# Moving the low-half subtractions of two MLPs from GpSimd to the vector engine, and keeping one step of weight preparation away from the sums

## The chip, the cores and the metric

One core of one Trainium2 chip runs the whole program. Times are device microseconds of an execution; the kernel before took 695.05 us (median of 3 runs, 694.81 to 695.08). Engines are named as the profile names them: PE (matrix products), PEld (its weight loads), DVE (vector engine), ACT (scalar engine), POOL (GpSimd), SP (issues the DMAs).

## The reference, cut to what is computed

```python
q_pool = q.reshape(B, H, S // 2, 2, D).mean(axis=3)            # B 2, H 8, S 1152, D 64
scores = scale * np.matmul(q_pool, k.transpose(0, 1, 3, 2))
attn = softmax(scores)
x = np.matmul(attn, v)  ->  (1152 tokens, 512)
h = x @ w_in            # 512 x 2048, first layer
g = h * np.tanh(log1p(exp(h)))                                 # Mish
x = g @ w_out           # 2048 x 512
h = x @ w_in2           # second layer
g = np.where(h > 0.0, h, np.exp(np.minimum(h, 0.0)) - 1.0)     # ELU
out = g @ w_out2
```

The products of the MLPs are made to nearly full single precision: each operand is cut into a high half in fp32r, which the PE multiplies fast, and a low half, the operand less its high half. Three products (high·high, low·high, high·low) are summed. The weights arrive as 8-byte words and are turned into single precision on the chip.

## The kernel before, in words

Attention runs first, then both MLPs in one loop (`mlps()`). The order on every engine is the order in which the Python code issues instructions; each engine works its own queue in that order and waits at an instruction until its inputs are there.

The MLPs' work is cut into 96 units, 48 for each layer: a unit is one chunk of 128 hidden columns for one block of 384 tokens. The chunks of a layer fall into three groups (6, 5, 5 in the first layer, 5, 5, 6 in the second), and a group is worked for all three token blocks before the next. Pass `u` of the loop issues, in this order:

- `h_mm(u)` (L174): 12 matmuls for the hidden values of unit u, into a bank A of PSUM.
- `out_mm(u-3)` (L570): the matmuls of unit u-3 into the output banks. In the second layer these are 9 matmuls, three into each of 3 banks.
- `finish(u-3)` (L589): only when unit u-3 is the last of its group and block. The **sums**: the output banks are added to `part` in SBUF (L612, on DVE) or copied there (L603 on ACT, L605 on DVE). The banks B, B, B, C, D are given out in turn, so in the second layer the third bank that the next group needs is the first one that these sums set free. "The sums of pass u" are those issued in pass u.
- `split(u-1)` (L564, second layer): ACT copies `g` to its high half `gh` (L567), POOL subtracts to get the low half `gl` (L568).
- `mish(u)` (L537) in the first layer: ACT makes `gh` and `g` (L542, L543), POOL makes `gl` (L544). `elu(u)` (L549) in the second: ACT makes `x`, `e`, `r` (L555 to L557), then DVE `e` (L559) and DVE `g` (L561).
- The steps of weight pieces that have reached their age (`advance`, L638). A piece is half a chunk's weights, 128 x 512. It is read by DMA in pass t; in pass t+2 ACT scales its words (`rebias`, L119) and POOL clamps them (`clamp`, L123); in pass t+3 DVE runs three **words** instructions (L128, L133, L134); in pass t+4 ACT makes the high half `wh` (L144); in pass t+5 POOL makes the low half `wl` (`rest`, L147).
- `between()` (L628): one left-over addition or subtraction of the first layer's result, on POOL.

When pieces are read is settled by a small planner (L520 to L531): every piece has a latest pass, from its chunk's first use, and pieces are read no closer than 1.5 passes apart unless that latest pass forces it. Pieces for the attention part go through the same class `Weights` in another loop (L481 to L495).

Of the kernel before, what the change touches and what calls it, by code (L numbers as in the profile page):

```python
# [16 lines left out]
ALU = mybir.AluOpType  # L17
# [5 lines left out]
def tile_pool_attention_mish_elu_mlp(  # L23
# [14 lines left out]
    nc = tc.nc  # L38
# [44 lines left out]
    class Weights:  # L83
# [59 lines left out]
            self.h, self.l = (t[:, part * DM:(part + 1) * DM] for t in wt[self.layer, self.c])  # L143
            nc.scalar.copy(self.h, self.f)  # L144

        def rest(self):
            nc.gpsimd.tensor_tensor(self.l, self.f, self.h, op=ALU.subtract)  # L147


    ps = ctx.enter_context(tc.tile_pool(name="ps", bufs=1, space=PSUM))  # L150
# [9 lines left out]
    units = []  # L160
# [25 lines left out]
    def attention():  # L186
        with ExitStack() as st:
# [122 lines left out]
            def qk(s, j):  # L310
                n, i = tiles[s]
                KA, KBt = ks[n]
                Q = qs_t[n]
                sc[s, j] = pt = psum("A")
                c = slice(j * KB, (j + 1) * KB)
                if order[i] is None:
                    cols = slice(NQ * P, NQ * P + P)
                    terms = [(Q[0, 0], KA), (Q[0, 1], KA), (Q[1, 0], KBt), (Q[1, 1], KBt)]
                else:
                    h, t = order[i]  # L320
                    cols = slice(t * P, (t + 1) * P)
                    terms = [(Q[h, 0], (KA, KBt)[h]), (Q[h, 1], (KA, KBt)[h])]
                for x, (qq, kk) in enumerate(terms):
                    nc.tensor.matmul(pt[:, :KB], qq[:, cols], kk[:, c], start=(x == 0), stop=(x == len(terms) - 1))  # L324
# [14 lines left out]
            def exp(s):  # L339
                m = stat[s]  # L340
                nc.scalar.activation(sp[s], sp[s], AF.Exp, bias=m[:, 3:4], scale=1.0, accum_out=m[:, 4:5])  # L341
# [95 lines left out]
            while s < len(tiles) or avs or going:  # L437
                o = s - LAG
                new, old = s < len(tiles), 0 <= o < len(tiles)
                mid = 0 <= s - 1 < len(tiles)  # L440
                now = avs.pop(s, [])
                for j in range(3):
                    if new:
                        qk(s, j)
                    if j == 3:
                        for a in now:
                            av(*a)
                    if s in preps and 1 == j:
                        f, n, g = preps.pop(s)
                        f(n, g)  # L450
                    if old:
                        trans(o, j)
                if 3 == 3:
                    for a in now:
                        av(*a)
                more = left["dve"] and not any(w.age == 3 for w in going)
                if mid:
                    exp(s - 1)
                leave("act")
                if old:  # L460
                    for j in range(3):
                        if j != 1 or not more:
                            probs(o, j, nc.scalar.copy)
                if new:
                    scores(s, 0)
                    scores(s, 1)
                if mid:
                    norm(s - 1)
                if new:
                    scores(s, 2)  # L470
                    top(s)
                leave("dve")
                leave("pool", most=2)
                if old and (1 in [j for _, j in tp]):
                    probs(o, 1, nc.vector.tensor_copy)
                for n, g, kt in now:
                    if kt == KT - 1:
                        tokens(n, g)
                if 2 <= s % NI < 2+2 and s // NI + 1 < n_pairs:
                    pool_q(s // NI + 1, nc.gpsimd, (s % NI - 2,))  # L480
                for w in list(going):  # L481
                    w.age += 1
                    if w.age == 2:
                        w.rebias()
                        w.clamp()
                    elif w.age == 3:
                        w.shift()
                    elif w.age == 4:
                        w.words()
                        if w.x >= NW:  # L490
                            going.remove(w)
                    elif w.age == 5:
                        w.high()
                        w.rest()
                        going.remove(w)  # L495
                for f in loads.pop(s, []):
                    f()
                if pieces and s >= 3 and s % 5 == 3:
                    going.append(Weights(*pieces.pop(0)))
                    going[-1].read()  # L500
                s += 1
# [3 lines left out]
    def mlps():  # L505
        with ExitStack() as st:
# [7 lines left out]
            AHEAD = 3  # L514
# [5 lines left out]
            last, t = [], len(units)  # L520
            for x, y in reversed(loads):
                ahead = 8 if x < NW + NF else 7
                t = min(first_use[x] - ahead + AHEAD * y, t - 1)
                last.append(t)
            last.reverse()
            when, t = [], -100.0
            for (x, y), end in zip(loads, last):
                room = last_use[x - RING] + AHEAD - 3 if x >= RING else 0
                t = end if x < NW + NF else min(end, max(t + 1.5, room))
                assert t >= room or x < NW + NF, (x, y)  # L530
                when.append(t)  # L531
            going, later = [], []
# [4 lines left out]
            def mish(u):  # L537

                h = hs.pop(u)[:, :TB]
                g = tmp("g")  # L540
                gh, gl = g_t[u] = halves()
                nc.scalar.activation(gh, h, AF.Mish)  # L542
                nc.scalar.activation(g, h, AF.Mish)  # L543
                nc.gpsimd.tensor_tensor(gl, g, gh, op=ALU.subtract)  # L544

            def halves():
                return tuple(mp.tile([P, TB], F32R, tag=t, name=t, bufs=AHEAD + 1) for t in ("gh", "gl"))
# [1 line left out]
            def elu(u):  # L549


                h = hs.pop(u)[:, :TB]
                x, e, t = tmp("x", 2), tmp("e", 2), tmp("r", 2)
                g = es[u] = tmp("g")
                nc.scalar.activation(x, h, AF.Relu, scale=-1.0)  # L555
                nc.scalar.activation(e, x, AF.Exp, scale=-1.0)
                nc.scalar.activation(t, x, AF.Tanh, scale=-0.5)  # L557
                yield
                nc.vector.scalar_tensor_tensor(e, e, 1.0, t, op0=ALU.add, op1=ALU.mult)  # L559
                yield  # L560
                nc.vector.tensor_tensor(g, e, h, op=ALU.max)  # L561
                yield

            def split(u):  # L564
                g = es.pop(u)
                gh, gl = g_t[u] = halves()
                nc.scalar.copy(gh, g)  # L567
                nc.gpsimd.tensor_tensor(gl, g, gh, op=ALU.subtract)  # L568

            def out_mm(u):  # L570
                layer, gi, blk, c, first, final = units[u]
# [66 lines left out]
            def advance(age, *steps):  # L638

                for g in list(going):  # L640
                    if g.age == age:
                        for f in steps:
                            getattr(g, f)()
                        if "rest" in steps:
                            going.remove(g)

            acts = {}

            def go(u):
                if u in acts:  # L650
                    next(acts[u], None)

            for u in range(min(0, int(when[0]) - 1), len(units) + AHEAD):
                for g in going:
                    g.age += 1
                w = u - AHEAD
                if 0 <= u < len(units):
                    h_mm(u)
                if 0 <= w < len(units):
                    out_mm(w)  # L660
                if 0 <= w < len(units):
                    finish(w)
                if u - 1 in es:
                    split(u - 1)
                if 0 <= u < len(units):
                    if units[u][0] == 0:
                        mish(u)
                    else:
                        acts[u] = elu(u)
                go(u)  # L670
                advance(5, "rest")
                go(u)
                advance(4, "high")
                go(u)
                advance(2, "rebias", "clamp")
                go(u)
                advance(3, "shift", "words")
                between()
                while loads and when[0] <= u:
                    x, y = loads[0]  # L680
                    if x >= RING and last_use[x - RING] + AHEAD > u + 3:
                        break
                    loads.pop(0)
                    when.pop(0)
                    g = Weights(x, y)
                    assert u + (2 if g.ready else 5) <= first_use[x] + AHEAD * y, (x, y, u)
                    going.append(g)
                    if g.ready:
                        g.age = 3
                    else:  # L690
                        g.read()
                    break
            assert not loads and not going and not later

    with tc.manual_schedule():
        attention()
        mlps()
# [29 lines left out]
```

## Time and profile before

| | us |
|---|---|
| runs shown, median (lowest to highest) | 695.05 (694.81 to 695.08) |
| the profiled execution's own time | 695.86 |
| its span, first to last instruction | 694.0 |
| PE busy | 673.9 (97%) |
| DVE busy | 475.9 (69%) |
| ACT busy | 434.0 (63%) |
| POOL busy | 408.5 (59%) |

The share of an engine is over the whole span, and the stages differ: attention takes the first 282 us, the first layer runs from there to about 476 us, the second to the end. The page's chain of waits, followed back from the last instruction, is 73% PE and 18% DVE. To find where PE is held up one reads the busy time by stretch, then PE's instructions in order of time around the one stretch in which its busy time falls short, then the engine named behind the gap.

### The profile page before, as it was taken

Reading aid. Unit: us, or ns where it says so; the run is one execution under the profiler, and the core shown is the slowest. Engines: PE = TensorE matmul, PEld = TensorE weight load, DVE = VectorE, ACT = ScalarE, POOL = GpSimd, SP = SyncE. Lnnn points to the kernel's source line nnn. Section 1 sums busy time; section 2 is a strip of 40 time slices with the busy share of each in tenths; the row PEclk is TensorE's granted clock in tenths of the full one; section 3 lists DMA queues with packets and bytes.
Section 4 is the critical chain, followed back from the end, with each engine's and each line's share of the span. In section 5 each row is a group of like instructions: output and inputs, shape, how many; then the busy total and the mean of one; then the engine's idle time right before and its main releaser. Section 6 shows DMA issues by size and latency. Waiting matters only on the chain.

```text
span 694.0 us, 11253 instructions
## 1 busy us (share of the span) xinstructions
PE 673.9 (97%) x3976; PEld 582.6 (84%) x3976; DVE 475.9 (69%) x1120; ACT 434.0 (63%) x896; POOL 408.5 (59%) x446
## 2 busy tenths in 40 slices
PE   6799999999999999999999999999999999979997
PEld 4677777777777776899999999999989999969996
DVE  5989889898898885001474455765888888895332
ACT  4898988887888787424354554445766666565442
POOL 3666666564646453624576797897775756664221
PEclk9999999999999999999999999999999999989999
DMA  7322232324140200110232222322222223200111
GB/s 200 100 66 69 65 101 65 111 62 128 62 124 9 89 9 1 62 31 32 91 122 92 63 90 91 92 92 61 91 61 92 92 70 102 72 31 1 46 46 45
DMA packets 47400, 50.79 MB, mean 73 GB/s; under 512 B 20336, under 2 KB 38256, under 8 KB 47344
## 3 DMA queue, kind: packets, MB, share of 16 engines
q1 hardware_dynamic: 47344, 50.08, 23.9%
q8 instruction: 31, 0.51, 0.3%
q14 instruction: 25, 0.20, 0.1%
HBM read 47.71 MB, written 2.36 MB: 72 GB/s over the span
## 4 chain that ended last, share of the span: by engine, by line
PE 73%; DVE 18%; issue 4%; ACT 2%; POOL 2%; DMA 0%; DVEq 0%; POOLq 0%
PE A L181 19%; PE A L324 13%; PE B L587 12%; PE C L378 11%; PE B L353 10%; DVE wf L134 4%; DVE e L559 4%; PE D L587 4%; PE C L587 3%; DVE wf L133 3%; DVE wf L128 2%; PE D L254 1%; DVE sp L330 1%; DVE part L612 1%; DVE g L561 1%
## 5 line engine op out<-in xcount | busy, mean ns | idle before, releaser
L347 POOL TENSOR_SCALAR sp<-sp,stat 128x1152 f32<-128x1152 f32 x72 | 89.3, 1240 | 107.1 <-DVE stat L346 67.4
L181 PE MATMUL A<-XH,wh 128*128 128x384 f32 x384 | 129.6, 337 | 0.0
L181 PE MATMUL A<-XH,wl 128*128 128x384 f32 x384 | 129.4, 337 | 0.0
L181 PE MATMUL A<-XL,wh 128*128 128x384 f32 x384 | 129.3, 337 | 0.0
L330 DVE TENSOR_SCALAR_CACHE_REDUCE sp<-A 128x384 f32<-128x384 f32 x216 | 114.3, 549 | 13.6 <-PE A L324 12.4
L353 PE MATMUL B<-ident,sp 128*128 128x128 f32 x648 | 105.7, 273 | 4.4 <-issue 2.2
L341 ACT ACTIVATE sp<-sp,stat 128x1152 f32<-128x1152 f32 x72 | 90.9, 1263 | 23.5 <-DVE stat L337 22.9
L568 POOL TENSOR_TENSOR gl<-g,gh 128x384 fp32r<-128x384 f32 x48 | 55.3, 1152 | 77.4 <-ACT gh L567 77.4
L353 PEld LDWEIGHTS B<-ident,sp 128*128 128x128 f32 x648 | 81.2, 140 | 13.8 <-issue 3.5
L544 POOL TENSOR_TENSOR gl<-g,gh 128x384 fp32r<-128x384 f32 x48 | 55.2, 1153 | 53.7 <-ACT g L543 53.1
L369 ACT COPY pt<-B 128x384 f32<-128x384 f32 x188 | 81.7, 484 | 7.7 <-PE B L353 6.3
L378 PE MATMUL C<-pt,vr 128*64 128x320 f32 (+1 forms) x576 | 85.1, 418 | 0.9 <-DVE XL L394 0.9
L128 DVE TENSOR_SCALAR wf<-wf 128x512 int32<-128x512 int32 x56 | 39.3, 702 | 66.0 <-POOL wf L123 65.8
L147 POOL TENSOR_TENSOR wl<-wf,wh 128x512 fp32r<-128x512 f32 x56 | 83.6, 1493 | 0.4 <-ACT wh L144 0.2
L559 DVE SCALAR_TENSOR_TENSOR e<-e,r 128x384 f32<-128x384 f32 x48 | 44.9, 935 | 48.1 <-ACT r L557 48.0
L181 PEld LDWEIGHTS A<-XH,wh 128*128 128x128 f32 x384 | 72.7, 189 | 2.5 <-issue 0.5
L181 PEld LDWEIGHTS A<-XL,wh 128*128 128x128 f32 x384 | 72.6, 189 | 2.0
L324 PE MATMUL A<-KA,Q 128*128 128x384 f32 x240 | 73.5, 390 | 0.3 <-DVE KA L259 0.2
L181 PEld LDWEIGHTS A<-XH,wl 128*128 128x128 f32 x384 | 72.6, 189 | 0.0
L324 PE MATMUL A<-KB,Q 128*128 128x384 f32 x240 | 71.1, 379 | 1.2 <-DVE sp L330 1.2
L134 DVE SCALAR_TENSOR_TENSOR wf<-raw,wf 128x512 int32<-128x512 int32 x56 | 68.8, 1228 | 1.9
L542 ACT ACTIVATE gh<-A 128x384 fp32r<-128x384 f32 x48 | 23.7, 493 | 69.6 <-PE A L181 69.6
(115 smaller groups left out, 1358.2 us busy)
## 6 DMA issues: line engine op xcount, KB each, us to landing
raw<-in_moe_w_in_dram SPq DMA_DIRECT2D x32, 512.0 KB, 3.8
raw<-in_moe_w_out_dram SPq DMA_DIRECT2D x32, 512.0 KB, 3.3
vr<-in_v_dram SPq DMA_DIRECT2D x8, 576.0 KB, 3.9
kr<-in_k_dram SPq DMA_DIRECT2D x14, 288.0 KB, 4.2
qr<-in_q_dram SPq DMA_DIRECT2D x7, 512.0 KB, 3.9
out_dram<-part SPq DMA_DIRECT2D x8, 256.0 KB, 2.2
kr<-in_k_dram SPq DMA_DIRECT2D x6, 96.0 KB, 3.1
qr<-in_q_dram SPq DMA_DIRECT2D x2, 256.0 KB, 3.3
```

The lines of the kernel that those rows point to most:

```text
L134: nc.vector.scalar_tensor_tensor(f, self.low, 29, f, op0=ALU.logical_shift_right, op1=ALU.bitwise_or)
L147: nc.gpsimd.tensor_tensor(self.l, self.f, self.h, op=ALU.subtract)
L181: nc.tensor.matmul(pt[:, :TB], w[:, kk * P:(kk + 1) * P], x[:, kk, tk], start=(i == 0), stop=(i == len(terms) - 1))
L324: nc.tensor.matmul(pt[:, :KB], qq[:, cols], kk[:, c], start=(x == 0), stop=(x == len(terms) - 1))
L330: nc.vector.tensor_scalar(sp[s][:, j * KB:(j + 1) * KB], sc.pop((s, j))[:, :KB], SCALE, None, op0=ALU.mult, op1=ALU.max, accum_out=stat[s] ...
L341: nc.scalar.activation(sp[s], sp[s], AF.Exp, bias=m[:, 3:4], scale=1.0, accum_out=m[:, 4:5])
L347: nc.gpsimd.tensor_scalar(sp[s], sp[s], m[:, 6:7], 1.0, op0=ALU.mult, op1=ALU.mult)
L353: nc.tensor.transpose(pt[:, x * P:(x + 1) * P], sp[s][:, c:c + P], ident)
L369: copy(dst, src)
L378: nc.tensor.matmul(acc[n, g][h * D:(h + 1) * D, :w], vs[n][:, h, kt, :], pts[n, g][:, kt, h, :], start=(kt == 0), stop=(kt == KT - 1),)
L559: nc.vector.scalar_tensor_tensor(e, e, 1.0, t, op0=ALU.add, op1=ALU.mult)
L587: nc.tensor.matmul(pt, l, r, start=(first and i == 0), stop=(final and i == 2))
```

## The change

POOL's subtractions inside `mlps()` go to DVE: `gl` in `mish` and in `split`, and `wl` in `rest`. In the attention part `rest` stays on POOL. In the first layer `gl` is issued at the end of a pass; in the second, `g` is issued before `rebias`, `clamp` and the words, with nothing between `e` and `g`. The planner gets a set `full` of passes; a piece whose reading pass falls in it, so that its words would be issued in the pass just ahead of the second layer's sums, is read one pass later if its latest pass allows that.

```diff
-        def rest(self):
-            nc.gpsimd.tensor_tensor(self.l, self.f, self.h, op=ALU.subtract)
+        def rest(self, eng=nc.vector):
+            eng.tensor_tensor(self.l, self.f, self.h, op=ALU.subtract)
...
                     elif w.age == 5:
                         w.high()
-                        w.rest()
+                        w.rest(nc.gpsimd)
...
+            full = {u + AHEAD - 4 for u in range(len(units)) if units[u][5] and units[u][0]}
             for (x, y), end in zip(loads, last):
                 room = last_use[x - RING] + AHEAD - 3 if x >= RING else 0
                 t = end if x < NW + NF else min(end, max(t + 1.5, room))
+                if np.ceil(t) in full and t + 1 <= end:
+                    t = np.ceil(t) + 1.0
...
                 nc.scalar.activation(g, h, AF.Mish)
-                nc.gpsimd.tensor_tensor(gl, g, gh, op=ALU.subtract)
+                yield
+                nc.vector.tensor_tensor(gl, g, gh, op=ALU.subtract)
...
                 nc.scalar.copy(gh, g)
-                nc.gpsimd.tensor_tensor(gl, g, gh, op=ALU.subtract)
+                nc.vector.tensor_tensor(gl, g, gh, op=ALU.subtract)
...
                 if 0 <= u < len(units):
-                    if units[u][0] == 0:
-                        mish(u)
-                    else:
-                        acts[u] = elu(u)
+                    acts[u] = (mish, elu)[units[u][0]](u)
                 go(u)
                 advance(5, "rest")
+                advance(4, "high")
+                if 0 <= u < len(units) and units[u][0]:
+                    go(u)
+                    go(u)
+                advance(2, "rebias", "clamp")
+                advance(3, "shift", "words")
                 go(u)
-                advance(4, "high")
-                go(u)
-                advance(2, "rebias", "clamp")
-                go(u)
-                advance(3, "shift", "words")
-                go(u)
                 between()
```

What that does to the order on the engines, at three places. In the changed file the lines of `elu`, `split` and `finish` stand four lower (L559 is L563, L561 is L565, L568 is L572, L612 is L616).

DVE from the words of pass 74 through the sums of pass 75 to the words of that pass, before:

```order
L128 TENSOR_SCALAR wf<-wf 128x512
L133 SCALAR_TENSOR_TENSOR wf<-raw,wf 128x512
L134 SCALAR_TENSOR_TENSOR wf<-raw,wf 128x512
L612 TENSOR_TENSOR part<-C,part 128x512
L612 TENSOR_TENSOR part<-D,part 128x512
L612 TENSOR_TENSOR part<-B,part 128x512
L559 SCALAR_TENSOR_TENSOR e<-e,r 128x384
L561 TENSOR_TENSOR g<-e,A 128x384
L128 TENSOR_SCALAR wf<-wf 128x512
L133 SCALAR_TENSOR_TENSOR wf<-raw,wf 128x512
L134 SCALAR_TENSOR_TENSOR wf<-raw,wf 128x512
```

The same place with the change:

```order
L128 TENSOR_SCALAR wf<-wf 128x512
L133 SCALAR_TENSOR_TENSOR wf<-raw,wf 128x512
L134 SCALAR_TENSOR_TENSOR wf<-raw,wf 128x512
L616 TENSOR_TENSOR part<-C,part 128x512
L616 TENSOR_TENSOR part<-D,part 128x512
L616 TENSOR_TENSOR part<-B,part 128x512
L572 TENSOR_TENSOR gl<-g,gh 128x384
L147 TENSOR_TENSOR wl<-wf,wh 128x512
L563 SCALAR_TENSOR_TENSOR e<-e,r 128x384
L565 TENSOR_TENSOR g<-e,A 128x384
L128 TENSOR_SCALAR wf<-wf 128x512
```

The two subtractions stand behind the sums and ahead of `e`. Here the words of pass 74 still stand just ahead of the sums: the latest pass of that piece does not allow the move, and the same holds for the words of pass 79 and the sums of pass 80.

DVE up to the sums of pass 60 (copies in the first group, L605), where a piece does move, before, from pass 58 on:

```order
L559 SCALAR_TENSOR_TENSOR e<-e,r 128x384
L561 TENSOR_TENSOR g<-e,A 128x384
L559 SCALAR_TENSOR_TENSOR e<-e,r 128x384
L561 TENSOR_TENSOR g<-e,A 128x384
L128 TENSOR_SCALAR wf<-wf 128x512
L133 SCALAR_TENSOR_TENSOR wf<-raw,wf 128x512
L134 SCALAR_TENSOR_TENSOR wf<-raw,wf 128x512
L605 COPY part<-D 128x512
L605 COPY part<-B 128x512
```

and with the change, from the words of pass 58 on:

```order
L128 TENSOR_SCALAR wf<-wf 128x512
L133 SCALAR_TENSOR_TENSOR wf<-raw,wf 128x512
L134 SCALAR_TENSOR_TENSOR wf<-raw,wf 128x512
L572 TENSOR_TENSOR gl<-g,gh 128x384
L147 TENSOR_TENSOR wl<-wf,wh 128x512
L563 SCALAR_TENSOR_TENSOR e<-e,r 128x384
L565 TENSOR_TENSOR g<-e,A 128x384
L609 COPY part<-D 128x512
L609 COPY part<-B 128x512
L572 TENSOR_TENSOR gl<-g,gh 128x384
L147 TENSOR_TENSOR wl<-wf,wh 128x512
```

The words of pass 59 have gone behind the sums; `gl` and `wl` of passes 59 and 60 have come in. Pieces move in the same way from ahead of the sums of passes 55 and 70.

POOL in the second layer, before:

```order
L123 TENSOR_SCALAR wf<-wf 128x512
L568 TENSOR_TENSOR gl<-g,gh 128x384
L147 TENSOR_TENSOR wl<-wf,wh 128x512
L123 TENSOR_SCALAR wf<-wf 128x512
L568 TENSOR_TENSOR gl<-g,gh 128x384 x2
```

and with the change, from the last of the first layer's left-over subtractions to the end:

```order
L640 TENSOR_TENSOR XL<-part,XH 128x384 x2
L123 TENSOR_SCALAR wf<-wf 128x512 x20
```

Of POOL's three kinds of instruction there only the clamp is left.

## Rows read from the trace of the kernel before

**Rows 1.** Busy time by engine, three stretches: span, PE, PEld, DVE, ACT, POOL; clock; DMA.

```profile
282.20:475.81 193.61, 193.61 (x1118) 193.56 (x1117) 87.94 (x94) 87.07 (x184) 135.40 (x124) 1.00 0.26 79
475.81:609.87 134.06, 134.06 (x683) 122.25 (x682) 112.70 (x140) 85.86 (x174) 90.73 (x80) 1.00 0.27 82
609.87:632.90 23.03, 19.27 (x85) 17.22 (x84) 18.98 (x23) 13.15 (x28) 14.05 (x13) 0.85 0.01 5
```

**Rows 2.** PE in order of time, units 75 to 83: start us, duration us, instruction.

```profile
593.09 0.33 PE L181 MATMUL A<-XH,wh 128*128 128x384 f32 x1
...
609.87 0.33 PE L181 MATMUL A<-XH,wh 128*128 128x384 f32 x1
...
612.67 0.39 PE L587 MATMUL B<-wh,gh 128*128 128x512 f32 x1
...
614.05 0.33 PE L181 MATMUL A<-XH,wh 128*128 128x384 f32 x1
...
617.31 0.40 PE L587 MATMUL B<-wh,gl 128*128 128x512 f32 x1
621.47 0.79 PE L587 MATMUL B<-wh,gh 128*128 128x512 f32 x1 [3.76 <-DVE part L612]
...
622.91 0.52 PE L181 MATMUL A<-XH,wh 128*128 128x384 f32 x1
...
628.71 0.33 PE L181 MATMUL A<-XH,wh 128*128 128x384 f32 x1
```

**Rows 3.** Busy time, the PE's gap and the 5 us behind it; PEclk is granted clock.

```profile
617.70:621.40 3.70, 0.01 (x1) 0.00 (x0) 3.60 (x7) 2.63 (x7) 2.44 (x2) 0.77 0.00 0
621.40:626.40 5.00, 4.93 (x14) 4.64 (x15) 3.03 (x6) 2.49 (x6) 3.19 (x4) 0.50 0.00 2
```

**Rows 4.** DVE in order of time, units 75 to 80.

```profile
595.78 0.68 DVE L612 TENSOR_TENSOR part<-C,part 128x512 f32<-128x512 f32 x1
596.38 0.67 DVE L612 TENSOR_TENSOR part<-D,part 128x512 f32<-128x512 f32 x1
...
601.21 1.65 DVE L559 SCALAR_TENSOR_TENSOR e<-e,r 128x384 f32<-128x384 f32 x1
...
603.36 0.77 DVE L128 TENSOR_SCALAR wf<-wf 128x512 int32<-128x512 int32 x1
...
620.74 1.27 DVE L612 TENSOR_TENSOR part<-B,part 128x512 f32<-128x512 f32 x2
```

**Rows 5.** POOL in order of time, the same stretch.

```profile
600.69 1.74 POOL L147 TENSOR_TENSOR wl<-wf,wh 128x512 fp32r<-128x512 f32 x1
603.23 0.62 POOL L123 TENSOR_SCALAR wf<-wf 128x512 f32<-128x512 f32 x1 [0.80 <-ACT wf L119]
```

**Rows 6.** DVE in order of time, units 53 to 55.

```profile
503.07 1.57 DVE L559 SCALAR_TENSOR_TENSOR e<-e,r 128x384 f32<-128x384 f32 x1 [1.94 <-ACT r L557]
...
507.85 0.69 DVE L134 SCALAR_TENSOR_TENSOR wf<-raw,wf 128x512 int32<-128x512 int32 x1
508.46 0.55 DVE L559 SCALAR_TENSOR_TENSOR e<-e,r 128x384 f32<-128x384 f32 x1
509.05 0.56 DVE L561 TENSOR_TENSOR g<-e,A 128x384 f32<-128x384 f32 x1
509.52 0.42 DVE L128 TENSOR_SCALAR wf<-wf 128x512 int32<-128x512 int32 x1
509.97 0.69 DVE L133 SCALAR_TENSOR_TENSOR wf<-raw,wf 128x512 int32<-128x512 int32 x1
510.70 1.39 DVE L134 SCALAR_TENSOR_TENSOR wf<-raw,wf 128x512 int32<-128x512 int32 x1
```

**Rows 7.** POOL's groups between 475.8 and 632.9: count, busy us, mean ns, idle.

```profile
L568 POOL TENSOR_TENSOR gl<-g,gh 128x384 fp32r<-128x384 f32 x35 | 42.1, 1202 | 39.2 <-ACT gh L567 39.2
L147 POOL TENSOR_TENSOR wl<-wf,wh 128x512 fp32r<-128x512 f32 x26 | 40.4, 1555 | 0.0
```

## The prediction, made before the changed kernel ran

> **What bounds the kernel now.** Start with the busy time by stretch [rows 1]. In the first layer (282.20 to 475.81) PE is busy 193.61 of 193.61 us, and in the second layer up to 609.87 again 134.06 of 134.06. There PE sets the pace, and nothing done to another engine can show unless it makes PE wait. Only in 609.87 to 632.90 is PE short: 19.27 of 23.03 us.
>
> PE's own instructions show what happens there [rows 2]. The rows with A<-XH,wh at these times are the first matmul of a unit. Unit 80 takes 614.05 - 609.87 = 4.18 us, which is the length of a unit of the second layer. Unit 81 takes 622.91 - 614.05 = 8.86, unit 82 takes 628.71 - 622.91 = 5.80. Against 4.18 each that is 4.68 + 1.62 = **6.30 us lost**. Of it 3.76 us is a gap before the third output bank of the pass; the row names DVE's sum (L612) as what ended it. The rest is the clock [rows 3]: over the gap the granted clock averages 0.77, and in the 5.0 us behind it 0.50, the 1.2 GHz level; PE had done nothing since 617.70. The first matmul of unit 82 takes 0.52 instead of 0.33 [rows 2].
>
> So the question is why the sums come late. Call T75 and T80 the moments when PE has finished passes 75 and 80: 593.09 and 614.05, the starts of the next units [rows 2]. DVE begins the sums of pass 75 at 595.78, 2.69 us after T75, and those of pass 80 at 620.74, 6.69 after T80 [rows 4]. Between the two lie three sums of 0.60 (595.78 to 596.38) and five passes of `e`, `g` and words: (24.96 - 1.80) / 5 = 4.63 us a pass, against PE's 4.18. DVE is late at 75 and falls behind by another 4.0.
>
> What makes it slow stands in two places. Alone, `e` takes 0.55, L128 0.42, L133 and L134 0.69 [rows 6]. The `e` at 601.21 takes 1.65 [rows 4] while POOL runs the `wl` of 600.69 until 602.43 [rows 5]: DVE does its work only when POOL is done.
>
> **The change part by part.**
>
> *Instructions that come to DVE.* 96 `gl` and 58 `wl` leave POOL, one `gl` a pass, a `wl` in most. Neither has run on DVE here. Below, the nearest rows are DVE's instructions of the same size with two SBUF inputs: `e` at 0.55 for 128x384, L133 and L134 at 0.69 for 128x512 [rows 6]. Above, POOL's own means, 1.20 and 1.56 [rows 7]. I take DVE's, the same engine and size. Followed by an instruction that does not need the result, the slot is shorter than the duration: 0.47 behind `g` (509.05 to 509.52) and 0.61 behind L134 (507.85 to 508.46). So 0.47 for `gl`, 0.61 for `wl`.
>
> *Instructions that lose their partner.* Slots alone [rows 6]: `e` 0.59, `g` 0.47, L128 0.45, L133 0.73, L134 0.61; the three words instructions together 1.79.
>
> *What is left on POOL.* Only the clamp, 0.62 [rows 5]. Its price for DVE is bounded by 0, if it falls beside `g` or waits itself, and by its own 0.62. The L128 at 603.36, begun under the clamp of 603.23, took 0.77 instead of 0.42 [rows 4 to 6]. I take that 0.35 for each pass with a clamp.
>
> The rule for this is in the Trainium skill, "SBUF — State Buffer", section "Who interferes with whom": a DVE instruction with two SBUF inputs and a GpSimd instruction that reads SBUF exclude each other, and the one that comes second waits for the whole of the first. The `e` above agrees: 1.22 us until POOL's end, then 0.43. It speaks against moving still more two-input instructions to DVE beside a clamp. By it every clamp could cost its whole length, 0.62; the sums of pass 80 would come 1.1 us later than worked out next, and still in time.
>
> *A full pass* (`gl`, `wl`, `e`, `g`, words, clamp) is then 0.47 + 0.61 + 0.59 + 0.47 + 1.79 + 0.35 = **4.28 us**, with two instructions more than the 4.63 of before.
>
> *Lateness at pass 75.* The sums of pass 70 now follow a pass without words, so DVE takes them as PE delivers them. From there to the sums of 75 it has five passes of `gl`, `e`, `g` (5 x 1.53), three `wl` (0.61) and four sets of words with clamp (2.14): 7.7 + 1.8 + 8.6 = 18.0 us, where PE takes 5 x 4.18 = 20.9. The wait for `r` behind `g`, 1.94 at 503.07 [rows 6], can leave DVE idle in the one pass without words, but `gl` and `wl` now fall into that hole; with all of it 20.0, still under 20.9. So DVE is there when PE is. PE finishes the first bank 1.38 us before the end of a pass (612.67 against 614.05 [rows 2]) and the last at its end; the sums are through about 0.75 after T75, a sum's 0.67 [rows 4] and the signal.
>
> *Lateness at pass 80.* Five full passes, the last without a clamp (pass 80 has no words): 5 x 4.28 - 0.35 = 21.05 against 20.9. The sums of pass 80 start about 0.9 after T80 instead of 6.69. PE needed the bank at 617.54 (617.31 and a slot of 0.23) and got going 0.73 after the sum's start (620.74 to 621.47); so a start by T80 + 2.76 costs nothing [rows 2, 4]. The room is 1.9 us.
>
> *What this gives.* The gap of 3.76 goes, and with PE not idle the clock stays, 2.54 more: **6.30 us**.
>
> *Edits at nothing.* In the first layer 48 `gl` (0.55) and 33 `wl` (0.69) add 49 us to DVE's 87.94 of 193.61 [rows 1]; `gl` is needed by PE three passes on. The attention part keeps its order. A piece that is read a pass later is used five passes after its words at the earliest. Of the late ones the nearest is the last chunk: PE needs its first `wl` from about T80 + 8.4; with the sums of 80 through at 0.9 + 1.8, a pass without words (2.14) and the next `gl` and `wl` (1.08), DVE has it at T80 + 5.9. If that cover went, PE would wait there next.
>
> *Sum.* The profiled execution took 695.86 (span 694.0), so 689.56 for it. The median shown is 0.81 lower, 695.05: **688.7 us**.
>
> **Rivals.**
>
> *B, part of the gap stays.* DVE has more to do per pass than I count. With dependent slots for the new instructions (0.59 as behind `e`, 0.73 as behind L133) and each clamp at its full 0.62, a full pass is 4.79; five less one clamp are 23.3, and the sums of 80 start at T80 + 3.2, 0.4 too late: 689.2. It decides from 4.65 us a pass. Should the gap be long enough for the clock to fall, up to 2.5 us come on top: 691.7. For it: words still stand ahead of the sums of 75 and 80. Against: the shorter slots stand in the rows.
>
> *C, no gain.* The planner's new rule doesn't do what it says where the gap is: the passes ahead of 75 and 80 keep their words. If the order mattered and not POOL, the gap would stay: about 695. Against: the chain of numbers above needs the planner only for pass 70.
>
> *D, slower.* The long durations are DVE's own and not POOL's doing. Then a pass keeps its 4.63 and gets `gl` and `wl` on top, 5.71; five are 28.5, and the sums of 80 start at T80 + 0.75 + 28.5 - 20.9 = 8.4 even if those of 75 are on time. PE then waits 5.6 instead of 3.76: 1.9 slower, 697.0. It decides from where the sums of 80 start later than T80 + 6.69, a pass of 5.37. The upper bounds of `gl` and `wl`, 1.20 and 1.56, lie on the same side: a pass of 5.96 and 697.9. Against it speaks that the same instructions take 0.55 and 0.69 when POOL is idle [rows 6].
>
> **How the numbers follow.** The forecast without a gap has 0.74, B 0.14, C 0.05, D 0.07. A measurement of this kernel tells about 0.2%, 1.4 us, from no change. Faster: the forecast and B, 0.88; the same: C, 0.05; slower: D, 0.07. The range takes the forecast and B: up to 691.7, where B ends with the clock fallen (the upper bounds of `gl` and `wl` lie beyond, with D); down to 687.9, as nothing but a few tenths of the other units can be had beyond 6.30. That leaves out C and D, 0.12, and a little of the tails.
>
> **What would show it.** PE's units 81 and 82 at 4.18 with no gap, PE short of no stretch, a granted clock of 1.00 behind 475.81. `e` at 0.55 and L134 at 0.69 throughout the second layer, apart from the ones beside a clamp; `gl` near 0.55 and `wl` near 0.69 on DVE. The sums of pass 80 within 2.8 us after PE's end of that pass. It would be wrong if a gap stands in PE at another sum or before a matmul that reads `wl`, or if DVE's full pass comes out above 4.65 us.

## The result, and the profile after

| | before | after |
|---|---|---|
| median of 4 runs each | 695.07 us | 689.28 us |
| lowest to highest | 694.81 to 696.01 | 689.25 to 690.33 |
| the profiled execution's own time | 695.86 | 689.30 |
| its span | 694.0 | 687.5 |
| DVE busy | 475.9 | 506.6 |
| POOL busy | 408.5 | 214.1 |

After to before is 0.9918, with a 95% interval of 0.9901 to 0.9935: the change makes the kernel 4.5 to 6.9 us faster. Forecast were 688.7 us, in a range of 687.9 to 691.7.

PE in order of time, units 80 to 82 of the changed kernel (start us, duration us, instruction), against [rows 2]:

```profile
609.63 0.33 PE L181 MATMUL A<-XH,wh 128*128 128x384 f32 x1
...
613.81 0.33 PE L181 MATMUL A<-XH,wh 128*128 128x384 f32 x1
...
618.00 0.33 PE L181 MATMUL A<-XH,wh 128*128 128x384 f32 x1
```

Unit 80 takes 4.18 us and unit 81 takes 4.19; the 8.86 and 5.80 of units 81 and 82 are gone. Busy time by stretch (span, PE, PEld, DVE, ACT, POOL, granted clock), against [rows 1]:

```profile
282.20:475.76 193.56, 193.56 (x1118) 193.56 (x1117) 114.76 (x175) 86.35 (x184) 38.54 (x45) 1.00 0.25 79
475.76:609.63 133.87, 133.87 (x683) 122.48 (x682) 113.23 (x195) 88.72 (x179) 21.42 (x29) 1.00 0.26 83
609.63:632.60 22.97, 22.97 (x118) 21.01 (x117) 18.67 (x34) 12.88 (x27) 0.62 (x1) 1.00 0.00 1
```

In the third stretch PE is now busy 22.97 of 22.97 us, at a granted clock of 1.00 instead of 0.85. From the first unit to the last there is no stretch of the MLPs in which PE waits. POOL has gone from 135 to 39 us in the first layer and from 90.7 to 21.4 in the second stretch. DVE has hardly more to do in the second stretch than before (113.2 against 112.7 us), though it does POOL's work besides; in the first layer it has 26.8 us more.

DVE, from the sums of pass 75 through one full pass to the next pass's `gl`, and the sums of pass 80, against [rows 4, 6]:

```profile
591.70 0.69 DVE L616 TENSOR_TENSOR part<-C,part 128x512 f32<-128x512 f32 x1
...
593.08 0.69 DVE L616 TENSOR_TENSOR part<-B,part 128x512 f32<-128x512 f32 x1
593.69 0.55 DVE L572 TENSOR_TENSOR gl<-g,gh 128x384 fp32r<-128x384 f32 x1
594.15 0.68 DVE L147 TENSOR_TENSOR wl<-wf,wh 128x512 fp32r<-128x512 f32 x1
594.76 0.55 DVE L563 SCALAR_TENSOR_TENSOR e<-e,r 128x384 f32<-128x384 f32 x1
595.34 0.55 DVE L565 TENSOR_TENSOR g<-e,A 128x384 f32<-128x384 f32 x1
595.81 0.71 DVE L128 TENSOR_SCALAR wf<-wf 128x512 int32<-128x512 int32 x1
596.56 0.69 DVE L133 SCALAR_TENSOR_TENSOR wf<-raw,wf 128x512 int32<-128x512 int32 x1
597.28 0.69 DVE L134 SCALAR_TENSOR_TENSOR wf<-raw,wf 128x512 int32<-128x512 int32 x1
597.89 0.55 DVE L572 TENSOR_TENSOR gl<-g,gh 128x384 fp32r<-128x384 f32 x1
...
614.42 1.28 DVE L616 TENSOR_TENSOR part<-B,part 128x512 f32<-128x512 f32 x2
```

PE ends pass 75 at 592.88 and pass 80 at 613.81. DVE takes the first sum of pass 75 before PE has ended, 1.18 us ahead, where it came 2.69 late. The full pass from `gl` to `gl` takes 597.89 - 593.69 = 4.20 us. The sums of pass 80 begin 0.61 after PE's end, where they came 6.69 late. What is left of the disturbance is the clamp on POOL:

```profile
595.63 0.62 POOL L123 TENSOR_SCALAR wf<-wf 128x512 f32<-128x512 f32 x1 [5.34 <-ACT wf L119]
```

It ends at 596.25, and the L128 begun at 595.81 takes 0.71 instead of 0.42. POOL's left-over subtractions for the first layer's result (L640) still run at the start of the second layer, too.

### The profile page after: what moved, and what is told of

It is laid out like the page before. It is cut to its first block, busy times and chain, and to the rows that moved or that the text cites. A ratio compares the mean times of both kernels' runs of the same rounds, so it can differ in the third digit from the quotient of the medians.

```text
span 687.5 us, 11218 instructions
## 1 busy us (share of the span) xinstructions
PE 671.4 (98%) x3976; PEld 581.1 (85%) x3976; DVE 506.6 (74%) x1274; ACT 433.1 (63%) x896; POOL 214.1 (31%) x292
## 4 chain that ended last, share of the span: by engine, by line
PE 94%; DVE 3%; issue 1%; DMA 0%; ACT 0%; POOL 0%
PE A L181 29%; PE B L591 18%; PE A L324 13%; PE C L378 11%; PE B L353 10%; PE D L591 6%; PE C L591 5%; PE D L254 1%; DVE sp L330 1%; PE D L269 0%; DMA qr<-in_q_dram 0%; DVE KB L259 0%; DVE KA L259 0%; DVE part L616 0%; DVE pt L369 0%
## 5 line engine op out<-in xcount | busy, mean ns | idle before, releaser
L123 POOL TENSOR_SCALAR wf<-wf 128x512 f32<-128x512 f32 x56 | 37.7, 673 | 264.8 <-ACT wf L119 238.1
L548 DVE TENSOR_TENSOR gl<-g,gh 128x384 fp32r<-128x384 f32 x48 | 31.2, 650 | 50.1 <-ACT g L546 49.9
L378 PEld LDWEIGHTS C<-pt,vr 128*64 128x64 f32 x576 | 35.1, 136 | 28.3 <-issue 10.6
L571 ACT CAST gh<-g 128x384 fp32r<-128x384 f32 x48 | 24.7, 514 | 47.3 <-DVE g L565 47.0
L324 PEld LDWEIGHTS A<-KA,Q 128*128 128x128 f32 x240 | 37.7, 196 | 17.5 <-issue 4.3
L324 PEld LDWEIGHTS A<-KB,Q 128*128 128x128 f32 x240 | 38.2, 193 | 14.3 <-issue 7.6
```

What stands on the lines that cost most here:

```text
L123: nc.gpsimd.tensor_scalar(self.f, self.f, HUGE, -HUGE, op0=ALU.min, op1=ALU.max)
L378: nc.tensor.matmul(acc[n, g][h * D:(h + 1) * D, :w], vs[n][:, h, kt, :], pts[n, g][:, kt, h, :], start=(kt == 0), stop=(kt == KT - 1),)
L548: nc.vector.tensor_tensor(gl, g, gh, op=ALU.subtract)
```

## The experiments

Theory 1 is the prediction's: POOL's subtractions hold DVE's instructions up, and the gap goes because they leave POOL. Theory 2 is the other half of the change: what counts is that words stand just ahead of the sums. A third question is the size of the room, from what lateness on PE waits, which decides between the forecast and rival B. Beside these runs the kernel before took 696.0 to 696.1 us (medians), so each ratio is to the runs of the kernel before beside it.

### 1. The change without the planner's rule

```diff
-            full = {u + AHEAD - 4 for u in range(len(units)) if units[u][5] and units[u][0]}
...
-                if np.ceil(t) in full and t + 1 <= end:
-                    t = np.ceil(t) + 1.0
```

> The change without the planner's rule: the subtractions are on DVE, but the words stand ahead of the sums of passes 55, 60 and 70 as before. Theory 1 (POOL's subtractions held DVE's instructions up, and their leaving is what takes the gap away): no gap in PE, a full DVE pass of 4.2 us, the sums of pass 80 begin within 1 us after PE's end of pass 80, time 689.3. Theory 2 (it is the place of the words ahead of the sums): a gap of 1 us or more before the third bank at pass 81, 691 or more.

689.30 us, ratio 0.9907 (0.9892 to 0.9922): the whole gain. DVE, the last word of pass 69 with the sums of pass 70 right behind it, and the first two sums of pass 80:

```profile
569.79 0.69 DVE L134 SCALAR_TENSOR_TENSOR wf<-raw,wf 128x512 int32<-128x512 int32 x1
570.93 2.08 DVE L613 TENSOR_TENSOR part<-B,part 128x512 f32<-128x512 f32 x3 [0.45 <-PE B L588]
...
614.11 1.28 DVE L613 TENSOR_TENSOR part<-B,part 128x512 f32<-128x512 f32 x2
```

The words of pass 69 stand ahead of the sums, and still DVE waits 0.45 us for PE there. With short instructions it gets through its words in time. The sums of pass 80 begin 0.13 us after PE's end (613.98), even 0.5 earlier than with the rule. So theory 2 doesn't hold for this kernel: beside the move the rule adds nothing.

### 2. The rule without the move to DVE

```diff
+            full = {u + AHEAD - 4 for u in range(len(units)) if units[u][5] and units[u][0]}
...
+                if np.ceil(t) in full and t + 1 <= end:
+                    t = np.ceil(t) + 1.0
```

> The kernel before with the planner's rule alone: POOL keeps its subtractions, the words move from ahead of the sums of passes 55, 60 and 70. Theory 1: DVE's pass from 75 to 80 stays at 4.6 us; the sums of pass 75 come about 1 us earlier than the 2.7 us late of before, those of pass 80 still 5 to 6 us late, the gap is 2.3 to 3.3 us instead of 3.76, time 693 to 695. Theory 2: the gap is gone or under 1 us, 689 to 690.

696.40 us, ratio 1.0009 (0.9999 to 1.0019): no gain at all, less than the 1 to 3 us that theory 1 had given it. DVE's first sums of passes 75 and 80, and PE's instructions that waited for them:

```profile
596.23 0.68 DVE L615 TENSOR_TENSOR part<-C,part 128x512 f32<-128x512 f32 x1
...
621.17 1.28 DVE L615 TENSOR_TENSOR part<-B,part 128x512 f32<-128x512 f32 x2
```

```profile
596.96 0.50 PE L590 MATMUL C<-wh,gh 128*128 128x512 f32 x1 [0.36 <-DVE part L615]
...
621.90 0.80 PE L590 MATMUL B<-wh,gh 128*128 128x512 f32 x1 [3.75 <-DVE part L615]
```

PE ends pass 75 at 592.94, so the sums come 3.29 us late, later than in the kernel before (2.69), and PE now waits 0.36 us there too. The sums of pass 70 did get on time (571.86, 0.15 ahead of PE's end). But the piece that left the pass ahead of them, and those behind it, went into the passes up to 75: DVE has four sets of words between the sums of 70 and 75 (L128 at 576.04, 583.77, 587.32 and 592.33) where it had three. The prediction had counted four sets there, and my expectation still put the sums of pass 75 earlier. From 75 to 80 DVE takes the same time as before (24.94 us from sums to sums, 24.96 before), and the gap is 3.75 us as before.

This run settles a third part of the change besides, the new places of `g`, `rebias` and `clamp` in the code: in the second layer the instructions of DVE, ACT and POOL stand here in the same order as in the changed kernel, but for the 48 `gl` and 25 `wl` that moved. So it differs from the changed kernel there in the move alone.

### 3 and 4. Half of the move

```diff
-        def rest(self, eng=nc.vector):
+        def rest(self, eng=nc.gpsimd):
```

> The change with only gl on DVE; wl stays on POOL. Theory 1: a wl of 1.30 us and the clamp still hold DVE; a full DVE pass (gl 0.47, e 0.59, g 0.47, words 1.79, clamp 0.35: 3.67, and up to 1.3 of waiting) is 4.5 to 5.0 us, so the sums of pass 80 begin 2.3 to 4.8 us after PE's end of pass 80, where 2.8 is the limit: a gap of 0 to 2 us, 689.3 to 693. Theory 2: no gap, 689.3.

689.74 us, ratio 0.9913 (0.9898 to 0.9928). DVE, an L133 of a full pass and the sums of pass 80; POOL, the `wl` beside that L133; PE, what waited for the sums:

```profile
601.61 1.67 DVE L133 SCALAR_TENSOR_TENSOR wf<-raw,wf 128x512 int32<-128x512 int32 x1
...
617.02 1.28 DVE L616 TENSOR_TENSOR part<-B,part 128x512 f32<-128x512 f32 x2
```

```profile
601.26 1.47 POOL L147 TENSOR_TENSOR wl<-wf,wh 128x512 fp32r<-128x512 f32 x1
```

```profile
617.76 0.50 PE L591 MATMUL B<-wh,gh 128*128 128x512 f32 x1 [0.17 <-DVE part L616]
```

L133 takes 1.67 us: it ends 0.55 behind the end of `wl` (602.73). The full pass is 4.63 us, the sums begin 3.09 us after PE's end of pass 80 (613.93), and PE waits: unit 81 takes 4.62 us (613.93 to 618.55), 0.43 more than 4.19. This is rival B, in small.

```diff
-                nc.vector.tensor_tensor(gl, g, gh, op=ALU.subtract)
+                nc.gpsimd.tensor_tensor(gl, g, gh, op=ALU.subtract)
```

> The change with only wl on DVE; gl stays on POOL. Theory 1: gl of 1.02 us and the clamp hold DVE; a full pass (wl 0.61, e 0.59, g 0.47, words 1.79, clamp 0.35: 3.81, and up to 1.0 of waiting) is 4.5 to 4.8 us, the sums of pass 80 begin 2.3 to 3.8 us after PE's end of pass 80: a gap of 0 to 1 us, 689.3 to 691. Theory 2: no gap, 689.3.

The edit stands in `mish` and in `split`. 689.37 us, ratio 0.9912 (0.9895 to 0.9928). DVE and POOL:

```profile
601.82 1.39 DVE L134 SCALAR_TENSOR_TENSOR wf<-raw,wf 128x512 int32<-128x512 int32 x1
```

```profile
601.12 1.55 POOL L572 TENSOR_TENSOR gl<-g,gh 128x384 fp32r<-128x384 f32 x1 [0.34 <-ACT gh L571]
```

Here `gl` on POOL (601.12 to 602.67) doubles one words instruction of each pass, L134 from 0.69 to 1.39. A full pass takes 4.45 us, the sums of pass 80 begin 2.34 us after PE's end (613.84), and PE does not wait. Either half of the move is enough for nearly all of the gain; both together bring room.

### 5. POOL keeps its work, DVE has it too

```diff
                 nc.vector.tensor_tensor(gl, g, gh, op=ALU.subtract)
+                nc.gpsimd.tensor_tensor(spare[:, :TB], g, gh, op=ALU.subtract)
...
                         if "rest" in steps:
+                            nc.gpsimd.tensor_tensor(spare, g.f, g.h, op=ALU.subtract)
```

> The change as it is, and beside it POOL runs the same subtractions once more into a spare tile that nobody reads: DVE has its new work and POOL its old one. Theory 1: DVE's instructions are held as before (e up to 1.65 us, L134 1.4), a full DVE pass is 5 to 6.5 us, the sums of pass 80 come 5 us late or more and others late too: 694 to 705, slower than the kernel before if the pass is over 5.4. Theory 2: nothing changes, 689.3.

The first line added stands in `mish` and in `split`; the line that allocates `spare` is left out above. 732.70 us, ratio 1.0526 (1.0496 to 1.0557): the direction of theory 1, and more than its 694 to 705. What PE waited for (total us, times, longest), and DVE's groups in the second layer (count, busy us, mean ns, idle):

```profile
PE B L594 <- DVE gl L574: 5.7, 5, 1.5
PE C L594 <- DVE part L619: 5.2, 2, 4.9
...
PE A L181 <- DVE wl L147: 2.4, 2, 1.5
```

```profile
L134 DVE SCALAR_TENSOR_TENSOR wf<-raw,wf 128x512 int32<-128x512 int32 x24 | 36.0, 1502 | 0.8
L147 DVE TENSOR_TENSOR wl<-wf,wh 128x512 fp32r<-128x512 f32 x26 | 29.3, 1128 | 0.0
...
L574 DVE TENSOR_TENSOR gl<-g,gh 128x384 fp32r<-128x384 f32 x33 | 24.1, 731 | 2.9 <-ACT gh L573 2.9
```

The mean of L134 is 1502 ns, where it is 692 alone; `wl` has 1128 and `gl` 731. DVE is busy 175 of 181 us in the second layer and becomes the bound: a full pass takes 6.0 us, and PE waits not only for sums but for `gl` and `wl` themselves, which the expectation had left out. The first layer is longer too, 201.2 us for 193.6. DVE's new work costs nothing only because POOL's old work is gone.

### 6. POOL writes and doesn't read

```diff
-                nc.gpsimd.tensor_tensor(gl, g, gh, op=ALU.subtract)
+                nc.gpsimd.memset(gl.bitcast(F32), 0.0)
...
-            nc.gpsimd.tensor_tensor(self.l, self.f, self.h, op=ALU.subtract)
+            if read:
+                nc.gpsimd.tensor_tensor(self.l, self.f, self.h, op=ALU.subtract)
+            else:
+                nc.gpsimd.memset(self.l.bitcast(F32), 0.0)
```

> The kernel before, with POOL's subtractions in the MLPs replaced by fills of gl and wl with zeros: the low halves of the MLPs are left out, POOL writes tiles of the same size and reads none. Theory 1 in the form that only POOL's reading holds DVE: e at 0.55, L134 at 0.69, a DVE pass of 3.3 to 3.6 us, no gap, 688.7 to 689.3, with the words still ahead of the sums. Theory 1 in the form that any work on POOL holds DVE: e above 1 us beside a fill. Theory 2: the gap stays, 693 or more.

The fill of `gl` stands in `mish` and in `split`, and `mlps()` calls `rest` with `read` off, so the kernel leaves the low halves out of its products. 689.97 us, the median of 689.38 and 690.56, ratio 0.9912 (0.9883 to 0.9941), and no gap: the gain is there with nothing moved to DVE and the words where they were. (In the longer one, which is the profiled one, the MLPs begin at 283.45 instead of 282.19; attention, which the edit doesn't touch, took that difference of 1.26.) DVE's groups in the second layer:

```profile
L128 DVE TENSOR_SCALAR wf<-wf 128x512 int32<-128x512 int32 x25 | 22.5, 902 | 1.9 <-POOL wf L123 1.9
L562 DVE SCALAR_TENSOR_TENSOR e<-e,r 128x384 f32<-128x384 f32 x37 | 21.8, 589 | 38.3 <-ACT r L560 38.1
...
L134 DVE SCALAR_TENSOR_TENSOR wf<-raw,wf 128x512 int32<-128x512 int32 x25 | 17.6, 704 | 0.9
```

`e` has a mean of 589 ns where it had 1053 in the kernel before, L134 704 where it had 1368. The fills are shorter than the subtractions, so one has to look where they do fall beside a two-input instruction. DVE and POOL at such a place:

```profile
608.83 0.69 DVE L134 SCALAR_TENSOR_TENSOR wf<-raw,wf 128x512 int32<-128x512 int32 x1
```

```profile
608.56 0.52 POOL L150 MEMSET wl<- 128x512 f32 x1
609.03 0.42 POOL L571 MEMSET gl<- 128x384 f32 x1
```

L134 runs under two fills and takes 0.69, as it does alone; so fills don't hold the two-input instructions. But L128, one input, one output, has gone up, to 902 from 546. DVE and POOL at one such place:

```profile
516.50 1.63 DVE L128 TENSOR_SCALAR wf<-wf 128x512 int32<-128x512 int32 x1
518.17 0.69 DVE L133 SCALAR_TENSOR_TENSOR wf<-raw,wf 128x512 int32<-128x512 int32 x1
518.89 0.69 DVE L134 SCALAR_TENSOR_TENSOR wf<-raw,wf 128x512 int32<-128x512 int32 x1
```

```profile
516.06 0.61 POOL L123 TENSOR_SCALAR wf<-wf 128x512 f32<-128x512 f32 x1 [1.12 <-ACT wf L119]
516.61 0.77 POOL L571 MEMSET gl<- 128x384 f32 x2
517.33 0.53 POOL L150 MEMSET wl<- 128x512 f32 x1
```

L128 begins under the clamp and ends at 518.13, 0.27 behind the end of the last of three fills (517.86). L133 and L134 behind it, with no POOL work beside them, take 0.69. So two kinds of instruction are held by different things: L128 by a fill as well as by the clamp, `e` and the words' two-input instructions by POOL instructions that read. The Trainium skill, "SBUF — State Buffer", section "Who interferes with whom", says it that way: two SBUF inputs exclude a GpSimd instruction that reads, and only the two-port forms, which `tensor_scalar` can take, exclude one that writes. The trace agrees, 0.69 and 1.63 us.

### 7. The second layer alone

```diff
+                nc.gpsimd.tensor_tensor(gl, g, gh, op=ALU.subtract)
                 yield
-                nc.vector.tensor_tensor(gl, g, gh, op=ALU.subtract)
...
-                            getattr(g, f)()
+                            g.rest(nc.gpsimd) if f == "rest" and u < NC * NB else getattr(g, f)()
```

> The change for the second layer alone: in the passes of the first layer gl and wl stay on POOL. PE had no gap in the first layer before, so the theory that only PE's waits count has 689.3 here too, no gap, units of 4.16 us in the first layer and 4.19 in the second. If shorter DVE and POOL work in the first layer carried something over (DVE late at the first passes of the second layer), a gap or a late sum at passes 50 to 55 and 690 or more.

The first hunk is in `mish`. 689.55 us, ratio 0.9912 (0.9891 to 0.9932); no gap, the sums of pass 80 at 0.61 after PE's end. The move in the first layer, 48 `gl` and 33 `wl`, is worth nothing, as the row of PE's busy time there said [rows 1].

### 8 to 10. The room, by added work

```diff
                 advance(3, "shift", "words")
                 go(u)
+                if 75 <= u < 80:
+                    for _ in range(1):
+                        nc.vector.tensor_tensor(spare[:, :P], part[:, 0, :P], part[:, 1, :P], op=ALU.subtract)
```

> The change with one more DVE subtraction of 128x128 behind the words of passes 75 to 79, a slot of about 0.21 us. Room theory: the sums of pass 80 begin 0.61 + 5 x 0.21 = 1.7 us after PE's end of pass 80, inside the room of 2.76: no gap, 689.3. If every bit of added DVE work shows in the time: 690.3.

The edit above is this one's, without the line that allocates `spare`; the next has the full width of 512, the last has it twice.

> The change with one more DVE subtraction of 128x512 (a slot of 0.61 us) behind the words of passes 75 to 79, into a spare tile. Room theory: the sums of pass 80 begin 0.61 us after PE's end of pass 80 now and may begin at 2.76; five times 0.61 put them at 3.7, so PE waits 0.9 us: 690.2, a little more if the clock falls. If the room is larger than worked out: no gap, 689.3. If the lateness does not add up pass by pass: no gap.

> The same with two more subtractions in each of the five passes. Room theory: the sums of pass 80 begin at 6.7 us after PE's end of pass 80, PE waits 3.9 us, and the granted clock falls as it did before: 695.5 to 696.0, the time of the kernel before, with POOL out of the way. If the clock fell for another reason than the gap: 693.2.

689.30, 690.35 and 696.46 us (ratios 0.9902, 0.9918, 1.0002). DVE's first sums of pass 80 with the small one, and with one more; then PE with one more, and with two more, and the clock in the 5 us behind that gap:

```profile
615.43 1.28 DVE L617 TENSOR_TENSOR part<-B,part 128x512 f32<-128x512 f32 x2
```

```profile
617.48 1.28 DVE L617 TENSOR_TENSOR part<-B,part 128x512 f32<-128x512 f32 x2
```

```profile
618.22 0.50 PE L592 MATMUL B<-wh,gh 128*128 128x512 f32 x1 [0.71 <-DVE part L617]
...
619.02 0.34 PE L181 MATMUL A<-XH,wh 128*128 128x384 f32 x1
```

```profile
621.85 0.80 PE L592 MATMUL B<-wh,gh 128*128 128x512 f32 x1 [4.18 <-DVE part L617]
...
623.30 0.52 PE L181 MATMUL A<-XH,wh 128*128 128x384 f32 x1
...
629.42 0.33 PE L181 MATMUL A<-XH,wh 128*128 128x384 f32 x1
```

```profile
621.80:626.80 5.00, 4.95 (x14) 4.66 (x15) 4.38 (x8) 1.62 (x4) 0.00 (x0) 0.50 0.01 2
```

The runs that tell of the room, in one table; the lateness is the start of the sums of pass 80 after PE's end of that pass, the loss is unit 81 over 4.19 us:

| run | lateness | gap in the row | loss in unit 81 | time |
|---|---|---|---|---|
| without the rule | 0.13 | none | 0 | 689.30 |
| after | 0.61 | none | 0 | 689.28 |
| one small more | 1.64 | none | 0 | 689.30 |
| only `wl` moved | 2.34 | none | 0 | 689.37 |
| only `gl` moved | 3.09 | 0.17 | 0.43 | 689.74 |
| one more | 3.62 | 0.71 | 0.97 | 690.35 |
| before | 6.69 | 3.76 | 4.67 | 695.07 (696.1 beside the others) |
| two more | 7.26 | 4.18 | 5.26 | 696.46 |

Lateness less loss is 2.66 and 2.65 in the two short cases: that is the room, forecast as 2.76. Work on DVE inside it is free, and in these two runs all the lateness beyond it is paid. Of the long gaps the rows show more: with two more the clock is 0.50 behind the gap and unit 82 takes 6.12 us (623.30 to 629.42), where it took 5.80 in the kernel before [rows 2, 3]; behind the gap of 0.71 unit 82 takes 4.18 (619.02 to 623.20). The expectation for two more had the sums 6.7 us late and 695.5 to 696.0 us, and both came out higher: a pair of added instructions takes 1.33 us a pass (614.53 to 615.86) and not twice 0.61. Two added instructions a pass put back the whole time of the kernel before, with POOL's subtractions out of the way, so DVE's lateness by itself is enough for that time.

## Why the prediction was right, point by point

**The bound.** PE sets the pace wherever it isn't held up, and the one large hold-up was the gap at unit 81 and the low clock behind it. Shown by the changed kernel's rows and by experiments 7 and 8 to 10.

**The cost of the moved instructions.** Taken as 0.55 and 0.69 with slots of 0.47 and 0.61; measured 0.55 and 0.68 with slots of 0.46 and 0.61 (593.69 to 594.15, 594.15 to 594.76). The lower bounds were the right ones.

**The clamp.** Taken as 0.35 of its 0.62; measured 0.29 at the L128 above.

**The full pass.** Forecast 4.28, measured 4.20.

**The lateness.** At pass 75 forecast as none, with the sums through 0.75 after PE's end; they were through at 593.77, 0.89 after. At pass 80 forecast 0.9, measured 0.61. The room was 2.65 instead of 2.76. So the margin was 2.0 us where 1.9 were forecast. One premise was not needed: that the sums of pass 70 follow a pass without words. In experiment 1 they follow words, and DVE still waits there for PE.

**The sum.** 6.30 us were forecast for the profiled executions, and they differ by 695.86 - 689.30 = 6.56. The rest is in other units that ran over before, 0.17 in unit 56 and some hundredths in unit 76 and ahead of the second layer; both units are at 4.18 to 4.19 now, and the prediction had spoken of a few tenths there and left them out of the sum. Within the 6.30 the prediction gave all of the 2.54 beyond the gap to the clock. The three short gaps (0.17, 0.36 and 0.71 us) leave the clock at 1.00 and still cost 0.26 more than the row's gap each (their units are 0.43, 0.62 and 0.97 over 4.19), so the clock's share is nearer to 2.3. The medians differ by 5.79. The step that was off is the last one: the profiled execution of before stood 0.81 over the median, and I took the same 0.81 from the changed kernel; but its profiled execution stands at its median, 689.30 against 689.28. What made the one stand over its median no run here shows. Hence 0.58 us of error in the forecast of 688.7.

**DVE in the first layer.** I added 49 us to the 87.94 of before, which makes 137; it is 114.8. The 87.94 contained waiting for POOL that goes as well: L134 has a mean of 741 ns in that stretch, where it had 1215. Nothing hung on it.

**Rival B** is real, and its threshold of 4.65 us a pass was near: with a pass of 4.63, only `gl` moved, PE waits. There the passes up to 75 are longer too, so that the same 4.63 gives more lateness than B had worked out from on-time sums.

**Rival C** was right in its first half. The rule does not act at passes 75 and 80, and experiments 1 and 2 show that it gives nothing: 689.30 without it, 696.40 with it alone. Its second half, that the gap would stay for that reason, was wrong.

**Rival D** falls. In the second layer all 24 L134 take 0.69, and 47 of the 48 `e` take 0.55 or 0.56; the one of 1.37 runs beside a left-over subtraction on POOL (L640, 489.90 to 491.35). They become long again when POOL reads beside them (experiment 5) and not when it fills (experiment 6).

## What to carry to other kernels

When two engines slow each other's instructions, work that is moved onto the busier of them can leave it hardly busier: in the second layer DVE took 48 `gl` and 25 `wl` from POOL, 44.3 us of work, and its busy time there rose by 3.1 us (from 152.97 to 156.07, from 475.8 to the end), 0.5 of it before 609.63. In the first layer it took 54.4 us of work and its busy time rose by 26.8. Compare the duration of the same instruction with and without the other engine's work beside it before counting the move as load. And ask of a late instruction how much lateness its reader can bear: half of this move brought all but 0.1 to 0.5 us, because it got inside a room of 2.65 us (only `wl` moved, 2.34) or just beyond it (only `gl`, 3.09).

## What the runs showed that I had not expected

- The rule alone made the sums of pass 75 later (3.29 us instead of 2.69) and opened a second gap of 0.36 us: a piece that makes room ahead of one group of sums crowds the next.
- L128 was held not by one POOL instruction but by a row of them: 1.63 us under a clamp and three fills that followed each other without a pause, while in the changed kernel, with the clamp alone, it takes 0.71. I had counted one POOL instruction's length as the most that a DVE instruction can wait.
- Gaps of 0.17 and 0.71 us in PE left the granted clock at 1.00, the 2.4 GHz level; behind the gaps of 3.76 and 4.18 it was at 0.50, the 1.2 GHz level. On top of the gap units 81 and 82 together lost 2.54 us in the kernel before and 3.01 with two more.
- With POOL's work doubled onto DVE and kept on POOL, the kernel was 36.6 us slower than the one before, six times the gain of the move: DVE was then the bound in the second layer (busy 175 of 181 us).
